# A spectral first stage: real bins folded into a product, projections turned by VectorE, weight conversion double-buffered

## The chip, the cores and the metric

The program runs on one core of one Trainium2 chip. The core has TensorE (PE in the profile; PEld is its weight load), VectorE (DVE), ScalarE (ACT), GpSimd (POOL), and SyncE (SP), whose queue issues most of the DMA transfers. Each engine works through its own instructions in the order in which the program gives them. The metric is the device time of one execution, in microseconds; lower is better.

## The reference

Three layers follow each other. The input x has 8 batches of 3072 positions with 256 channels.

```
X  = rfft(x, axis=1)                                   # 1537 complex bins
Yr = soft(Xr @ w_r - Xi @ w_i + b_r)                   # soft(v) = sign(v) * max(|v| - 0.01, 0)
Yi = soft(Xr @ w_i + Xi @ w_r + b_i)
x  = irfft(Yr + 1j * Yi, n=3072).reshape(24576, 256)

logits = x @ phi                                       # 32 slots, 8 experts of 4 slots
slots  = softmax(logits, axis=0).T @ x                 # each slot: a mean over all tokens
slots  = relu(slots @ w1[e]) @ w2[e]                   # its expert
x      = softmax(logits, axis=1) @ slots

h   = x @ w_in                                         # 256 -> 2048
out = (h * tanh(softplus(h))) @ w_out                  # 2048 -> 256
```

moe2_w_in and moe2_w_out arrive as 64-bit floats, and the kernel converts them to 32-bit floats itself.

## The kernel before

The program has two halves. The last one, `ffn`, computes the third layer over all 24576 tokens and depends on the slots of all batches. The first half, which the change touches, computes the spectra, the logits and the slots. `body` writes it as small functions; each call gets a position by `at(position, function, ...)`, and all calls are issued sorted by position. That list sets the order on every engine. The unit of position is one k: there are 32 of them, four to a batch (k = 4b + g), each one 16 of a batch's 64 frequency groups. PSUM tiles come from one ring of eight buffers.

For one k the steps are these. `stage2` (position k - 1.1, thus two units ahead of what else is issued there) makes 768 spectral columns in four calls: 16 TensorE products into PSUM; ScalarE writes the rounded upper part `xh` and the real part, VectorE the rest `xl` and the sum of real and imaginary parts `xsum`. When half the channels are there, ScalarE rounds `xsum` and VectorE takes the rest, waiting for it. `linear` (k + i/6, i = 0 to 5, for two halves `eh` of the outputs) is the complex product done with three real ones, each of six matmuls; product m = 0 takes the sums and is kept in `k1`, and m = 1, 2 go through VectorE (`p` L247, `cl` L249) and GpSimd (L250) into the thresholded spectrum `yt`. `special` (k + 1.02, once in a batch) does bin 0 and the middle bin, which have no imaginary part and share one column: four more products for each `eh` from a tile `xs` of two columns, then three small VectorE operations.

`project` (k + 1.18) multiplies `yt` by `phi`, eight small products of 32 output rows. `ptrans` (k + 1.38) turns the result, `inv1` (k + 1.58) multiplies it by the inverse transform's first factor, and `uturn` (k + 1.78) turns that and sends it to DRAM as `udr`. Each turn is `turn`: two TensorE transposes into PSUM and a ScalarE copy out; `project` and `inv1` are each followed by a ScalarE copy too. `c_load` (4b + 4.78) reads `udr` back for a batch's logits `lps` at 4b + 5.17, from which softmax and slots follow. `ytrans` (L310) turns the spectrum itself for the slots.

Between these steps `conv` converts the 64-bit weights in 32 pieces; step 0 is the DMA load of a piece into `cvs` (one buffer), step 1 begins with VectorE's `cva` (L490) and GpSimd's `cvc` (L489). `xsplit` (L170, L171) prepares the input for `stage1` (L187) of the next batch.

Of the kernel before, what the change touches and what calls it, by code (L numbers as in the profile page):

```python
# [20 lines left out]
NP = 32  # L21
NS = 32
# [44 lines left out]
def body(ctx, tc, x, w_r, w_i, b_r, b_i, phi, w1, w2, w_in, w_out, cbig, ct, out, dbg=None, stop=False):  # L67
    nc = tc.nc
# [51 lines left out]
    x_t, b_t, xh_t, xl_t, xs_t, yt_t, y_t, pt_t, k1_t = {}, {}, {}, {}, {}, {}, {}, {}, {}  # L120
# [81 lines left out]
    def stage2(k, h, p0):  # L202
        b, g = divmod(k, 4)
        if h == 0 and p0 == 0:
            xh_t[k] = bp.tile([128, 2, 8, 3, 48], F32R, tag="xh", name="xh")
            xl_t[k] = bp.tile([128, 2, 8, 3, 48], F32R, tag="xl", name="xl")
            if g == 0:
                xs_t[k] = sm.tile([128, 2, 2], F32, tag="xs", name="xs")
# [4 lines left out]
        xh = xh_t[k][:, h, p0:p0 + 4, 0:2]  # L213
        nc.scalar.activation(out=xh, in_=ps, func=AF.Copy)  # L214
        if p0 == 0:
            k1_t["s", h] = lp.tile([128, 8, 48], F32, tag="xsum", name="xsum")
        xs = k1_t["s", h]
        nc.scalar.activation(out=xs[:, p0:p0 + 4], in_=ps[:, :, 0], func=AF.Copy)  # L218
        nc.vector.tensor_sub(xl_t[k][:, h, p0:p0 + 4, 0:2], ps, xh.bitcast(F32))  # L219
        nc.vector.tensor_add(xs[:, p0:p0 + 4], ps[:, :, 1], xs[:, p0:p0 + 4])  # L220
        if g == 0 and p0 == 0:
            nc.vector.tensor_copy(xs_t[k][:, h, :], ps[:, 0, 0:2, 47])
        if p0 == 4:
            xh = xh_t[k][:, h, :, 2]
            nc.scalar.activation(out=xh, in_=xs, func=AF.Copy)  # L225
            nc.vector.tensor_sub(xl_t[k][:, h, :, 2], xs, xh.bitcast(F32))

    def linear(k, eh, m):
# [5 lines left out]
        ps = psum([128, 8, 48], "l")  # L234
        es = slice(eh * 128, eh * 128 + 128)
        n = 0
        for h in range(2):
            for w, xx in ((wh, xh), (wh, xl), (wl, xh)):
                nc.tensor.matmul(ps, lhsT=w[:, h, es], rhs=xx[:, h, :, src, :], start=n == 0, stop=n == 5)  # L239
                n += 1  # L240
        if m == 0:
            k1_t[eh] = lp.tile([128, 8, 48], F32, tag="k1", name="k1")
            nc.scalar.activation(out=k1_t[eh], in_=ps, func=AF.Copy)
# [8 lines left out]
    def special(k, eh):  # L252
        ps = psum([128, 2], "sp")
        for n, (h, w) in enumerate(((0, 0), (0, 1), (1, 0), (1, 1))):
            nc.tensor.matmul(ps, lhsT=wsp["a"][w].bitcast(F32)[:, h, eh * 128:eh * 128 + 128], rhs=xs_t[k][:, h, :],
                             start=n == 0, stop=n == 3)
        cl = sm.tile([128, 2], F32, tag="cs", name="cs")
        nc.vector.tensor_scalar(cl, ps, tlo[:, 0, eh:eh + 1], thi[:, 0, eh:eh + 1], op0=ALU.max, op1=ALU.min)
        nc.vector.tensor_sub(cl, ps, cl)
        nc.vector.tensor_scalar(yt_t[k][:, eh, 0, :, 47], cl, 0.5, None, op0=ALU.mult)  # L260

    def project(k):
        yt = yt_t[k]
        ps = psum([128, 2, 96], "pp")
        for eh in range(2):
            for j in range(4):
                nc.tensor.matmul(ps[32 * j:32 * j + 32], lhsT=ph[:, eh, :],
                                 rhs=yt[:, eh, 2 * j:2 * j + 2].rearrange("p q r f -> p q (r f)"),
                                 start=eh == 0, stop=eh == 1, tile_position=(0, 32 * j))
        pt = cp.tile([128, 2, 96], F32, tag="pt", bufs=2, name="pt")  # L270
        nc.scalar.activation(out=pt, in_=ps, func=AF.Copy)
        pt_t[k] = pt

    def turn(src, tag):
        ps = psum([96, 2, 128], "tn")
        for i in range(2):
            nc.tensor.transpose(ps[:, i], src[:, i], ident)  # L277
        t = cp.tile([96, 2, 128], F32, tag=tag, bufs=2, name=tag)
        nc.scalar.activation(out=t, in_=ps, func=AF.Copy)
        return t  # L280

    def ptrans(k):
        pt_t[k] = turn(pt_t[k], "phat")

    def inv1(k):
        g = k % 4
        ps = psum([128, 2, 96], "iu")
        for i in range(2):
            for j in range(4):
                nc.tensor.matmul(ps[32 * j:32 * j + 32, i], lhsT=pt_t[k][:, i, 32 * j:32 * j + 32],  # L290
                                 rhs=t_t[:, 8 * g + 2 * j + i, :], start=True, stop=True, tile_position=(0, 32 * j))
        ut = cp.tile([128, 2, 96], F32, tag="pt", bufs=2, name="ut")
        nc.scalar.activation(out=ut, in_=ps, func=AF.Copy)
        pt_t[k] = ut

    def uturn(k):
        b, g = divmod(k, 4)
        u = turn(pt_t.pop(k), "u")
        if g == 0:
            udr[b] = dram.tile([NP, 96, NS], F32, tag="udr", bufs=2, name="udr")  # L300
        dst = udr[b][8 * g:8 * g + 8].rearrange("(j i) p s -> i p j s", i=2)
        for i in range(2):
            nc.sync.dma_start(out=dst[i], in_=u[:, i].rearrange("p (j s) -> p j s", s=NS))
# [548 lines left out]
```

## Time and profile before

| | |
|---|---|
| time before, median of 3 runs | 2021.65 us (2021.46 to 2022.32) |
| time of the profiled execution | 2021.28 us |
| its span, first to last instruction | 2019.5 us |
| TensorE busy | 1939.8 us (96%) |
| VectorE busy | 1302.8 us (65%) |
| ScalarE busy | 872.1 us (43%) |
| GpSimd busy | 269.8 us (13%) |
| mean granted TensorE clock | 0.979 |

The profiled execution lies 0.37 us under the median, and 1.78 us of it are outside the span. A share of the whole span mixes the first half, up to about 700 us, and `ffn`, which begins with its first product at 749.5 us. A matmul's end is modelled, so consecutive matmuls overlap in the rows: what one costs is the distance from its start to the next start.

### The profile page before, as it was taken

The numbers are of one execution on the slowest core, as the hardware profiler recorded it, in microseconds if no ns is written. First come the engines' busy times: TensorE is split into PE (matmuls) and PEld (weight loads), VectorE is DVE, ScalarE is ACT, GpSimd is POOL, SyncE is SP. The second block draws the span as 40 slices with busy tenths as digits, with TensorE's granted clock in tenths as the row PEclk, the third lists the DMA queues.
The fourth block names the chain that finished last, engine by engine and source line by source line (L and its number), as shares of the span: only waits on it lengthen the run. The fifth ranks groups of instructions, "written<-read, shape, count | busy, mean of one in ns | idle before, by whom it ended". The sixth has DMA issues, their size and how long they took to land.

```text
span 2019.5 us, 31863 instructions
## 1 busy us (share of the span) xinstructions
PE 1939.8 (96%) x12670; PEld 1645.8 (81%) x12670; DVE 1302.8 (65%) x2020; ACT 872.1 (43%) x1569; POOL 269.8 (13%) x289
## 2 busy tenths in 40 slices
PE   5899999999999878999999999999999999999999
PEld 3787787888888647888888888888888888888887
DVE  3777767678777525666666666666666666666665
ACT  4566565565655422333333333333333333333332
POOL 1444343434434100000000000000000000000000
PEclk8999999899999899999999999999999999999999
DMA  8665465656664591002002001002001002000000
GB/s 250 177 181 159 147 179 153 176 158 177 194 185 118 192 326 42 22 22 53 22 22 53 22 21 42 22 22 53 21 22 53 22 22 53 21 22 22 22 22 21
DMA packets 147716, 177.16 MB, mean 88 GB/s; under 512 B 57504, under 2 KB 102688, under 8 KB 147120
## 3 DMA queue, kind: packets, MB, share of 16 engines
q1 hardware_dynamic: 145776, 170.38, 28.5%
q0 software_dynamic: 1792, 4.76, 0.7%
q8 instruction: 100, 1.64, 0.4%
q14 instruction: 48, 0.39, 0.1%
HBM read 103.79 MB, written 71.30 MB: 87 GB/s over the span
## 4 chain that ended last, share of the span: by engine, by line
PE 66%; DMA 3%; DVE 2%; issue 1%; ACT 1%; POOL 0%; SPq 0%; POOLq 0%; DVEq 0%; ACTq 0%
PE o L792 53%; PE h L762 9%; PE l L239 2%; DMA whl<-whl_d 1%; PE s L211 1%; DMA c_d<-chl 0%; DMA raw<-in_moe_w_dram 0%; PE tr L310 0%; POOL yt L250 0%; PE dt L436 0%; DVE rm L333 0%; PE tn L277 0%; PE dps L402 0%; DMA v<-udr 0%; PE sps L457 0%
## 5 line engine op out<-in xcount | busy, mean ns | idle before, releaser
L792 PE MATMUL o<-whl,gh 128*128 128x512 f32 x3072 | 1084.3, 395 | 8.5 <-DMA whl<-whl_d 8.5
L792 PE MATMUL o<-whl,gl 128*128 128x256 f32 x3072 | 828.4, 280 | 0.0
L768 ACT ACTIVATE g<-h 128x1024 f32<-128x1024 f32 x384 | 394.1, 1027 | 760.2 <-PE h L762 754.1
L792 PEld LDWEIGHTS o<-whl,gh 128*128 128x128 f32 x3072 | 567.2, 188 | 130.5 <-issue 8.9
L792 PEld LDWEIGHTS o<-whl,gl 128*128 128x128 f32 x3072 | 579.2, 189 | 31.5
L773 DVE CAST gh<-g 128x1024 fp32r<-128x1024 f32 x384 | 265.3, 691 | 366.9 <-ACT g L768 366.9
L777 DVE TENSOR_TENSOR gl<-g,gh 128x1024 fp32r<-128x1024 f32 x384 | 469.8, 1224 | 28.9 <-DVE gh L773 0.9
L762 PE MATMUL h<-ctt,mst 128*128 128x512 f32 x768 | 241.0, 395 | 2.1 <-ACT g L768 1.4
L250 POOL TENSOR_TENSOR yt<-p,cl 128x384 f32<-128x384 f32 x126 | 134.1, 1064 | 223.4 <-DVE cl L249 116.0
L762 PEld LDWEIGHTS h<-ctt,mst 128*128 128x128 f32 x768 | 121.0, 188 | 21.0 <-ACT g L768 2.3
L211 PEld LDWEIGHTS s<-tall,bt 96*128 96x128 f32 x1024 | 125.5, 201 | 6.3 <-DMA bt<-sdr 5.6
L211 PE MATMUL s<-tall,bt 96*128 96x96 f32 x1024 | 125.5, 283 | 4.5 <-DMA bt<-sdr 4.5
L187 PE MATMUL s<-xsp,f1s 128*128 128x512 f32 x288 | 100.8, 452 | 29.3 <-ACT xsp L170 13.4
L800 DVE TENSOR_TENSOR os<-o,os 128x256 f32<-128x256 f32 x192 | 76.2, 417 | 77.3 <-ACT os L799 77.3
L187 PEld LDWEIGHTS s<-xsp,f1s 128*128 128x128 f32 x288 | 53.2, 202 | 52.1 <-ACT xsp L170 19.3
L249 DVE TENSOR_SCALAR cl<-p,tlo,thi 128x384 f32<-128x384 f32 x128 | 75.6, 591 | 25.0 <-POOL yt L250 14.5
L799 ACT ACTIVATE os<-o 128x256 f32<-128x256 f32 x192 | 73.4, 383 | 41.0 <-PE o L792 38.0
L247 DVE TENSOR_TENSOR p<-l,k 128x384 f32<-128x384 f32 x128 | 70.4, 550 | 26.1 <-PE l L239 24.9
L219 DVE TENSOR_TENSOR xl<-s,xh 128x384 fp32r<-128x384 f32 x128 | 70.4, 550 | 18.4 <-ACT xsum L218 16.2
L214 ACT ACTIVATE xh<-s 128x384 fp32r<-128x384 f32 x128 | 62.3, 487 | 32.3 <-PE s L211 32.3
L225 ACT ACTIVATE xh<-xsum 128x384 fp32r<-128x384 f32 x64 | 33.5, 524 | 98.7 <-DVE xsum L220 98.7
L312 ACT ACTIVATE y<-tr 96x512 f32<-96x512 f32 x128 | 66.8, 599 | 17.7 <-PE tr L310 17.6
(189 smaller groups left out, 1919.0 us busy)
## 6 DMA issues: line engine op xcount, KB each, us to landing
xc<-in_x_dram SPq DMA_DIRECT2D x96, 256.0 KB, 3.1
sdr<-a SPq DMA_DIRECT2D x96, 256.0 KB, 3.4
bt<-sdr SPq DMA_DIRECT2D x32, 768.0 KB, 7.3
out_dram<-os SPq DMA_DIRECT2D x48, 512.0 KB, 2.6
ctt<-c_d SPq DMA_DIRECT2D x32, 384.0 KB, 7.8
c_d<-chl SPq DMA_DIRECT2D x16, 384.0 KB, 3.3
w1t<-in_moe_w_dram SPq DMA_DIRECT2D x6, 1024.0 KB, 6.9
w2t<-in_moe_w_dram SPq DMA_DIRECT2D x5, 1024.0 KB, 10.4
```

Of the source, the lines that this page charges most:

```text
L187: nc.tensor.matmul(ps, lhsT=f1s[w], rhs=xs[:, v], start=n == 0, stop=n == 2)
L211: nc.tensor.matmul(ps[:, i], lhsT=b_t[k][:, p0 + i, h * 128:(h + 1) * 128], rhs=t_m[:, 8 * g + p0 + i, :], start=True, stop=True)
L219: nc.vector.tensor_sub(xl_t[k][:, h, p0:p0 + 4, 0:2], ps, xh.bitcast(F32))
L249: nc.vector.tensor_scalar(cl, p, tlo[:, ri, eh:eh + 1], thi[:, ri, eh:eh + 1], op0=ALU.max, op1=ALU.min)
L250: (nc.vector if k == NK - 1 and m == 2 else nc.gpsimd).tensor_sub(yt[:, eh, :, ri, :], p, cl)
L762: nc.tensor.matmul(ps[:, i], lhsT=mst[:, f * 128:f * 128 + 128], rhs=ct_t[b][:, 4 * m:4 * m + 4].rearrange("p n t -> p (n t)"), start=True ...
L768: nc.scalar.activation(out=g, in_=h_t.pop(p), func=AF.Mish)
L773: nc.vector.tensor_copy(gh, g)
L777: nc.vector.tensor_sub(gl, g, gh.bitcast(F32))
L792: nc.tensor.matmul(o, lhsT=a[:, i, ts], rhs=w, start=f == 0 and n == 0, stop=f == 15 and n == 1)
L799: nc.scalar.activation(out=os[:, t], in_=ps[:, 1], func=AF.Copy)
L800: nc.vector.tensor_add(os[:, t], ps[:, 0], os[:, t])
```

## The change

Three edits, all in the first half.

1. The two real bins ride in the product of the sums. The tiles `xh`, `xl` are laid out by source (`NC` = 384 columns each of real, imaginary and sum), the sums have two more columns for the first unit of a batch, and `linear` with m = 0 multiplies 386 columns there. `special` reads the two columns from `k1`, without products of its own, and stands at k + 0.98 and 0.99.
2. `project` makes an output of 96 rows (three row blocks `a` of 32 frequencies) by 8 groups of 32 slots, with six products of 256 columns in place of eight of 192. One VectorE transpose of 32x32 blocks reads it from PSUM and writes `phat`; a second one does the same behind `inv1`. `turn`, `ptrans`, `uturn` and four ScalarE copies go. `inv1` stands at k + 1.48, and `udr` is written by four DMAs of 32 partitions, not two of 96.
3. `cvs` has two buffers, and step 0 of `conv` stands 0.45 of a piece ahead of step 1's piece (a piece is 0.953 units), where it stood 0.02 of a unit ahead. The tile `cvf` goes; `cva` takes its place.

```
     def linear(k, eh, m):
...
+        w = NC + 2 if m == 0 and k % 4 == 0 else NC
+        full = psum([128, NC + 2], "l")
+        ps = full[:, 0:w]
+        cs = slice(src * NC, src * NC + w)
...
-                nc.tensor.matmul(ps, lhsT=w[:, h, es], rhs=xx[:, h, :, src, :], start=n == 0, stop=n == 5)
+                nc.tensor.matmul(ps, lhsT=ww[:, h, es], rhs=xx[:, h, cs], start=n == 0, stop=n == 5)
...
     def special(k, eh):
-        ps = psum([128, 2], "sp")
-        for n, (h, w) in enumerate(((0, 0), (0, 1), (1, 0), (1, 1))):
-            nc.tensor.matmul(ps, lhsT=wsp["a"][w].bitcast(F32)[:, h, eh * 128:eh * 128 + 128], rhs=xs_t[k][:, h, :],
-                             start=n == 0, stop=n == 3)
+        v = k1_t[eh][:, NC:NC + 2]
...
     def project(k):
         yt = yt_t[k]
-        ps = psum([128, 2, 96], "pp")
+        ps = psum([96, 8, NS], "pp")
         for eh in range(2):
-            for j in range(4):
-                nc.tensor.matmul(ps[32 * j:32 * j + 32], lhsT=ph[:, eh, :],
-                                 rhs=yt[:, eh, 2 * j:2 * j + 2].rearrange("p q r f -> p q (r f)"),
-                                 start=eh == 0, stop=eh == 1, tile_position=(0, 32 * j))
-        pt = cp.tile([128, 2, 96], F32, tag="pt", bufs=2, name="pt")
-        nc.scalar.activation(out=pt, in_=ps, func=AF.Copy)
-        pt_t[k] = pt
...
+            v = yt[:, eh].rearrange("p q r f -> p q (r f)")
+            for a in range(3):
+                nc.tensor.matmul(ps[32 * a:32 * a + 32], lhsT=ph[:, eh, :], rhs=v[:, :, 32 * a:32 * a + 32],
+                                 start=eh == 0, stop=eh == 1, tile_position=(0, 32 * a))
+        pt_t[k] = cp.tile([96, 8, NS], F32, tag="phat", bufs=2, name="phat")
+        nc.vector.transpose(out=pt_t[k].rearrange("p q s -> p (q s)"), in_=ps.rearrange("p q s -> p (q s)"))
 
     def inv1(k):
...
-        ut = cp.tile([128, 2, 96], F32, tag="pt", bufs=2, name="ut")
-        nc.scalar.activation(out=ut, in_=ps, func=AF.Copy)
...
+        u = cp.tile([128, 2, 3, NS], F32, tag="u", bufs=2, name="u")
+        nc.vector.transpose(out=u.rearrange("p i a s -> p (i a s)"), in_=ps.rearrange("p i f -> p (i f)"))
...
-        for i in range(2):
-            nc.sync.dma_start(out=dst[i], in_=u[:, i].rearrange("p (j s) -> p j s", s=NS))
+        for j in range(4):
+            q = 8 * g + 2 * j
+            nc.sync.dma_start(out=udr[b][q:q + 2].rearrange("i (a n) s -> n i a s", n=32), in_=u[32 * j:32 * j + 32])
...
-            src = cvp.tile([128, n, 2], I32, tag="cs", name="cvs")
-            nc.sync.dma_start(out=src, in_=srcd[i])
-            cv.update(lo=src[:, :, 0].bitcast(U32), hi=src[:, :, 1])
+            cv["n"] = cvp.tile([128, n, 2], I32, tag="cs", bufs=2, name="cvs")
+            nc.sync.dma_start(out=cv["n"], in_=srcd[i])
...
-            at(k + 1.02, special, k, 0)
-            at(k + 1.03, special, k, 1)
+            at(k + 0.98, special, k, 0)
+            at(k + 0.99, special, k, 1)
         at(k + PA["pj"], project, k)
-        at(k + PA["pj"] + 0.2, ptrans, k)
-        at(k + PA["pj"] + 0.4, inv1, k)
-        at(k + PA["pj"] + 0.6, uturn, k)
+        at(k + PA["pj"] + 0.3, inv1, k)
...
-        at(sp * i - 0.02, conv, s_, d_, ii, 0)
+        at(sp * (i - 0.45), conv, s_, d_, ii, 0)
```

How this moves instructions is shown for unit k = 21, a second unit of a batch. On TensorE before, between `project` (`pp`) and the inverse product (`iu`) stood the transposes of the spectrum (`tr`), three groups of matmuls of `linear` (`l`), one of `stage1` (`s`), and the turn `tn`:

```order
L267 MATMUL pp<-yt,ph 32x192 x8
L310 MATMUL tr<-cb,yt 96x128 x16
...
L277 MATMUL tn<-cb,pt 96x128 x2
L187 MATMUL s_6341<-xsp,f1s_113 128x512
...
L436 MATMUL dt<-tall,dd 32x96 x8
L239 MATMUL l<-xh,ah 128x384
...
L436 MATMUL dt<-tall,dd 32x96 x8
L290 MATMUL iu<-tall,phat 32x96 x8
```

The same place of the changed kernel:

```order
L274 MATMUL pp<-yt,ph 32x256 x6
L300 MATMUL tr<-cb,yt 96x128 x16
L248 MATMUL l<-xh,ch 128x384
...
L248 MATMUL l<-xh,cl 128x384
L188 MATMUL s_6036<-xsp,f1s_113 128x512
...
L426 MATMUL dt<-tall,dd 32x96 x8
L285 MATMUL iu<-tall,phat 32x96 x8
L248 MATMUL l<-xh,ah 128x384
```

The turn is gone, and `iu` has moved ahead of the next six `l`; only one group of `l` and what stands with it now lies between `pp` and `iu`. On VectorE before, this unit's stretch ended the work of `stage2` (`xl`, `xsum`) and went on with two steps of `conv`, `p`, `cl` and more conversion:

```order
L226 TENSOR_TENSOR xl<-xsum,xh 128x8x48
L490 TENSOR_SCALAR cva<-cvs 128x256
L492 SCALAR_TENSOR_TENSOR cvb<-cvs,cva 128x256
L247 TENSOR_TENSOR p<-l,k_6245 128x384
L249 TENSOR_SCALAR cl<-p,tlo,thi 128x384
L494 SCALAR_TENSOR_TENSOR cvf<-cvc,cvb 128x256
```

The same place of the changed kernel:

```order
L232 TENSOR_TENSOR xl<-xsum,xh 128x384
L480 TENSOR_SCALAR cva<-cvs 128x256
L482 SCALAR_TENSOR_TENSOR cvb<-cvs,cva 128x256
L256 TENSOR_TENSOR p<-l,k_5946 128x384
L258 TENSOR_SCALAR cl<-p,tlo,thi 128x384
L277 STREAM_TRANSPOSE phat<-pp 96x256
L484 SCALAR_TENSOR_TENSOR cva<-cvc,cvb 128x256
L256 TENSOR_TENSOR p<-l,k_5946 128x384
L258 TENSOR_SCALAR cl<-p,tlo,thi 128x384
```

The transpose that `iu` needs stands behind `cl` of the next unit's first product, and so behind all of the work of `stage2` before it.

## Rows read from the trace of the kernel before

**Rows 1.** Stretch: length, busy PE, PEld, DVE, ACT, POOL, granted clock, DMA share, GB/s.

```profile
62.00:678.00 616.00, 588.28 (x5050) 503.59 (x5049) 464.79 (x964) 358.09 (x892) 262.07 (x277) 0.97 0.58 165
```

**Rows 2.** TensorE's waits, 62 to 678 us: total us, times, longest.

```profile
PE s L187 <- DVE xsp L171: 4.3, 3, 3.3
PE mt L340 <- DVE rm L335: 3.9, 4, 1.2
PE pp L267 <- DVE yt L260: 3.5, 2, 1.8
...
PE tn L277 <- ACT ut L293: 2.1, 1, 2.1
...
PE iu L290 <- ACT phat L279: 1.6, 1, 1.6
```

**Rows 3.** TensorE in order of time, the products of special (L255).

```profile
309.72 0.28 PE L255 MATMUL sp<-xs,ah 128*128 128x2 f32 x2
...
311.42 0.42 PE L239 MATMUL l<-xh,bh 128*128 128x384 f32 x1
```

**Rows 4.** TensorE in order of time around one turn (L277).

```profile
675.53 0.39 PE L277 MATMUL tn<-cb,ut 128*96 128x128 f32 x2
675.67 0.42 PE L239 MATMUL l<-xh,ch 128*128 128x384 f32 x1
675.93 0.34 PE L239 MATMUL l<-xl,ch 128*128 128x384 f32 x1
676.12 0.34 PE L239 MATMUL l<-xh,cl 128*128 128x384 f32 x1
```

**Rows 5.** TensorE in order of time, two kinds of products of 32 output rows.

```profile
335.45 0.86 PE L267 MATMUL pp<-yt,ph 128*32 128x192 f32 x16
...
683.37 3.66 PE L457 MATMUL sps<-y,dh 96*32 96x256 f32 x64
```

**Rows 6.** Groups of VectorE instructions by line: busy us, mean ns.

```profile
L220 DVE TENSOR_TENSOR xsum<-s,xsum 128x192 f32<-128x192 f32 x128 | 44.2, 345 | 0.0
...
L800 DVE TENSOR_TENSOR os<-o,os 128x256 f32<-128x256 f32 x192 | 76.2, 417 | 77.3 <-ACT os L799 77.3
...
L498 DVE SCALAR_TENSOR_TENSOR cvc<-cvs,cva 128x256 f32<-128x256 uint32 x32 | 19.7, 615 | 0.3
```

**Rows 7.** What VectorE waited for from 62 to 678 us.

```profile
DVE xl L226 <- ACT xh L225: 36.0, 61, 0.6
DVE cva L490 <- DMA cvs<-in_moe_w_in_dram: 25.4, 10, 3.9
...
DVE cva L490 <- DMA cvs<-in_moe_w_out_dram: 8.6, 6, 4.7
```

**Rows 8.** In order of time, TensorE's last `l`, `dt`, and VectorE's `cl`, in two units.

```profile
133.70 0.34 PE L239 MATMUL l<-xh,cl 128*128 128x384 f32 x1
...
133.73 0.48 DVE L249 TENSOR_SCALAR cl<-p,tlo,thi 128x384 f32<-128x384 f32 x1
...
656.78 0.34 PE L239 MATMUL l<-xh,cl 128*128 128x384 f32 x1
...
657.99 0.54 PE L436 MATMUL dt<-tall,dd 96*32 96x96 f32 x16
...
658.82 0.48 DVE L249 TENSOR_SCALAR cl<-p,tlo,thi 128x384 f32<-128x384 f32 x1
```

**Rows 9.** In order of time, one wait for a conversion load and the matmul behind it.

```profile
385.08 0.29 DVE L490 TENSOR_SCALAR cva<-cvs 128x256 int32<-128x256 int32 x1 [4.69 <-DMA cvs<-in_moe_w_out_dram]
...
388.22 0.80 PE L187 MATMUL s<-xsp,f1s 128*128 128x512 f32 x1 [3.29 <-DVE xsp L171]
```

**Rows 10.** Busy time by stretches, behind that wait; the columns of Rows 1.

```profile
387.00:407.30 20.30, 19.08 (x72) 17.84 (x72) 11.87 (x28) 5.55 (x14) 6.07 (x7) 0.50 0.50 134
```

**Rows 11.** The chain that ended last, behind the last unit's `project`.

```profile
679.22 0.57 PE pp L267 x8
...
683.05 0.33 SPq L303
```

More of the change, by code (lines that the diff above doesn't have):

```diff
@@ L21 @@
 NP = 32
+NC = 384
 NS = 32
@@ L212, in stage2, with part @@
                              start=True, stop=True)
-        xh = xh_t[k][:, h, p0:p0 + 4, 0:2]
+        def part(t):
+            v = t[:, h, 0:2 * NC].rearrange("p (r q f) -> p q r f", r=2, f=48)
+            return v[:, p0:p0 + 4]
+        xh = part(xh_t[k])
         nc.scalar.activation(out=xh, in_=ps, func=AF.Copy)
         if p0 == 0:
-            k1_t["s", h] = lp.tile([128, 8, 48], F32, tag="xsum", name="xsum")
+            k1_t["s", h] = lp.tile([128, NC + 2], F32, tag="xsum", name="xsum")
         xs = k1_t["s", h]
-        nc.scalar.activation(out=xs[:, p0:p0 + 4], in_=ps[:, :, 0], func=AF.Copy)
-        nc.vector.tensor_sub(xl_t[k][:, h, p0:p0 + 4, 0:2], ps, xh.bitcast(F32))
-        nc.vector.tensor_add(xs[:, p0:p0 + 4], ps[:, :, 1], xs[:, p0:p0 + 4])
+        xv = xs[:, 0:NC].rearrange("p (q f) -> p q f", f=48)[:, p0:p0 + 4]
+        nc.scalar.activation(out=xv, in_=ps[:, :, 0], func=AF.Copy)
+        nc.vector.tensor_sub(part(xl_t[k]), ps, xh.bitcast(F32))
+        nc.vector.tensor_add(xv, ps[:, :, 1], xv)
         if g == 0 and p0 == 0:
-            nc.vector.tensor_copy(xs_t[k][:, h, :], ps[:, 0, 0:2, 47])
+            nc.vector.tensor_copy(xs[:, NC:n], ps[:, 0, 0:2, 47])
         if p0 == 4:
-            xh = xh_t[k][:, h, :, 2]
-            nc.scalar.activation(out=xh, in_=xs, func=AF.Copy)
-            nc.vector.tensor_sub(xl_t[k][:, h, :, 2], xs, xh.bitcast(F32))
+            xh = xh_t[k][:, h, 2 * NC:2 * NC + n]
+            nc.scalar.activation(out=xh, in_=xs[:, 0:n], func=AF.Copy)
+            nc.vector.tensor_sub(xl_t[k][:, h, 2 * NC:2 * NC + n], xs[:, 0:n], xh.bitcast(F32))
     def linear(k, eh, m):
@@ L237, in linear @@
         for h in range(2):
[L238 to L239 removed]
+            for ww, xx in ((wh, xh), (wh, xl), (wl, xh)):
+                nc.tensor.matmul(ps, lhsT=ww[:, h, es], rhs=xx[:, h, cs], start=n == 0, stop=n == 5)
                 n += 1
         if m == 0:
[L242 to L243 removed]
+            k1_t[eh] = lp.tile([128, NC + 2], F32, tag="k1", name="k1")
+            nc.scalar.activation(out=k1_t[eh][:, 0:w], in_=ps, func=AF.Copy)
             return
```

48 lines of the change are left out of this document (17 added, 31 removed).

## The prediction

> **What bounds the kernel now.** I read the busy time by stretches first. From 62 to 678 us, the part of the first half in which units follow each other, TensorE is busy for 588.28 of 616.00 us, VectorE for 464.79 and ScalarE for 358.09 [rows 1]. So TensorE sets the end of this stretch, and of the stretch behind it too: `ffn` cannot begin before the last batch's slots. What TensorE's stream loses here, the end loses, one for one. The rest of TensorE's time, 27.7 us, is waiting, and the waits show for whom: mostly VectorE (`xsp`, `rm`, `yt`), some ScalarE in the two turns (`ut`, `phat`) [rows 2]. VectorE is nearer to its limit than its busy time tells: it also sits idle for 36.0 us inside `stage2`, where `xl` waits for ScalarE's rounding, and for 25.4 + 8.6 = 34.0 us at the head of conversion pieces, where `cva` waits for its load [rows 7]. Taken together it is occupied for 535 of 616 us, and it lags behind TensorE in bursts. A unit lasts 616.00 / 31 = 19.9 us, since 31 projections lie in this stretch.
>
> **What goes from TensorE.** Products of `special`: from their first row to the next `l` it is 311.42 - 309.72 = 1.70 us [rows 3], eight times: **-13.6 us**. In their place 12 matmuls in a batch have 386 columns in place of 384, some 0.01 us in all by the 0.19 us that one takes. Turns: the two transposes cost 675.67 - 675.53 = 0.14 us, and the matmul behind them 0.26 us to its successor in place of the 0.19 of the one after it [rows 4], thus 0.21 us for each of 64 turns: **-13.4 us**. The transposes' own busy time overlaps with their neighbours and is not what they cost.
>
> **What TensorE gets.** `project` goes from four rounds of four 192-column products (eight, in two passes each; 0.86 us with the tail) to four rounds of three 256-column ones. The nearest row with 256 columns is `sps`: 64 in 3.66 us, 0.229 us for a round of four [rows 5]. Lower bound 4 x 0.229 = 0.91 us, that is +0.05; upper bound the ratio of columns, 0.86 x 256 / 192 = 1.15, that is +0.29. I take the middle, +0.17 us, for 31: **+5.3 us** (bounds 1.6 and 9.0). The sum for TensorE's own work is -21.7 us.
>
> **What VectorE gets.** Two transposes for each unit, out of PSUM, of 256 and 192 columns. The trace has no VectorE transpose. By rows with as many columns and a PSUM operand they take 417 and 345 ns; the slowest row of 256 columns, 615 ns, bounds both from above, and below the 345 of the smaller one there is no reason to go [rows 6]. I take 0.76 us for a unit, 23.6 us in the stretch. ScalarE's four copies go; it was not the bound, and what their absence brings is the wait for ScalarE in the turns [rows 2]. For this transpose only the Trainium skill has a price: VectorE: DVE Perf Modes, section "The three transpose paths", gives 311 ns for 128x128 bf16, which by its 0.96 GHz clock and one column a cycle I estimate as 0.44 and 0.38 us here, 25.5 us in all; no run here shows it yet, and the sum would not change by it.
>
> VectorE gives back more than that: the load of `cvs` now leaves about 0.45 x 0.953 + 0.11 = 0.53 units (10.6 us) ahead of `cva`, where it left 0.13 units (2.5 us) ahead, and the second buffer lets it. The 34.0 us of waits [rows 7] should all but go. SP issues two DMAs more in a unit, by 0.33 us each [rows 11]; behind them in its queue are the loads `xc`, which are two steps of `stage1` ahead of their use and hide them. Without that cover it would be 0.7 us a unit.
>
> **The new wait.** `iu` needs `phat`, and `phat` now stands in VectorE's queue behind `xl`, `xsum` of `stage2` and `p`, `cl` of the next unit. On TensorE only `tr`, six `l` and in some units `s` and `dt` stand between `pp` and `iu`. Who waits behind it: all of TensorE. I compared in every unit when TensorE is through with these (what stands before `iu` now) and when VectorE is through with `cl`, plus 0.45 us for the transpose. In ten of the units between k = 3 and k = 29 VectorE is later. In k = 3 the last `l` starts at 133.70 and has its 0.19, and `cl` ends at 134.21: 0.8 us late. In k = 29 the last `l` starts at 656.78, `dt` then takes some 0.5, and `cl` ends at 659.30: 2.3 us [rows 8]. Over the ten it is 14.4 us. All are second and fourth units of a batch; in the first and third TensorE has softmax or slot products there as well. Two corrections about cancel: in three of the ten, 4.9 of the 14.4 us, a conversion wait stands shortly before, while TensorE comes earlier and VectorE has more to do in the second units, whose first unit holds the softmax reductions. So **+14.4 us**, bounds 0 and twice that. In the first units `mt` already waits for VectorE's `rm` [rows 2]; there TensorE arrives 1.7 us earlier for lack of `special`, and in half of the batches, where no conversion wait held VectorE up, that is lost again: **+5 us** with the edge of what `phat` adds.
>
> **Waits that go.** Behind conversion loads: the 3.3 of `xsp` and the 3.5 of `yt`; of the turns the 2.1 and 1.6 [rows 2]: **-10.5 us**. All waits together: +8.9 us.
>
> **The clock.** At 385.08 VectorE had waited 4.69 us for a load, and TensorE for that 3.29 us [rows 9]; behind it TensorE's granted clock is 0.50, thus 1.2 GHz, until 407.3 us, where 2.4 GHz is full speed [rows 10]. TensorE was busy for 19.08 us in these 20.30, so that full clock would have saved near half, 9.5 us. With the load early this cause goes, but a wait for `phat` may do the same elsewhere; I count half, **-5 us**.
>
> **Behind the last unit** the chain from `pp` to the `udr` transfer holds two turns and two copies: 683.05 - 679.22 = 3.8 us [rows 11], of which `iu` and `pp` are 1.2. Two transposes replace 2.6 us by 0.8, and two more DMA issues of 0.33 us come last: **-1 us**.
>
> **Sum.** -13.6 - 13.4 + 5.3 + 8.9 - 5 - 1 = -18.8 us on the profiled 2021.28 us; from the median, 0.37 higher, 2002.9 us. I predict **2003 us**. A change under 0.2% (4 us) is about what a measurement of this kernel cannot tell from none.
>
> **Rivals.**
>
> *The clock pays for the new wait.* A wait of 2 to 3 us in the second units is as long as the one that was followed by 20.30 us at 0.50 [rows 9, 10]. If two such stretches come and none goes, the clock costs +19 in place of -5: 2027 us; with one, 2013 to 2018 us. For it: the length. Against: the mean granted clock of the whole stretch is 0.97 [rows 1], so most waits were followed by no drop. The Trainium skill, TensorE: Matmul & The Clock Gate, section "HAM oscillation — how this bites in real kernels", says that idle gaps between bursts put the clock back to half; by that rule this rival gains, and the one stretch shown agrees.
>
> *VectorE's queue becomes the bound (slower).* If `iu` waits w us in every one of the 31 units, the sum without the clock is -21.7 - 1 - 10.5 + 31 w; it turns positive at w = 1.07 us. At 1.5 us it is +13.3: 2035 us. For it: VectorE's 535 us, less 34.0, plus 23.6, are 524 of the 594 us that TensorE would leave, and if a transpose took twice its price, 548. Against: my ten units are a third of all, a mean of 0.46 us, and each wait lets VectorE catch up.
>
> *The waits vanish (faster).* If the early loads leave VectorE no backlog at `stage2`, `iu` waits for nothing and the low stretch goes: -21.7 - 1 - 10.5 - 9.5 = -42.7: 1979 us. For it: 34.0 us of idle time given back against 23.6 of work. Against: ten lags remain of which only three have a load wait ahead.
>
> *The loads come no earlier* because SP reaches them late: waits stay, -21.7 - 1 + 14.4 + 5 - 3.7 (the turns' waits) = -7.0: 2015 us.
>
> **Chances.** The forecast, 1992 to 2010 us: 0.58. Waits vanish, below 1992: 0.20. Clock or loads, 2010 to 2017.6: 0.10. Between 2017.6 and 2025.7: 0.04. Slower by VectorE's queue or by two low stretches: 0.08. So faster 0.88, same 0.04, slower 0.08. The range takes three quarters of the case below and most of that above: 1982 to 2016 us; the forecast's own is 1992 to 2010.
>
> **What would show it.** In the trace after: no L255 products, no wait of `cva` for a load, VectorE's transposes at 0.35 to 0.62 us, `pp` rounds of 0.22 us and more, and under TensorE's waits a new line, `iu` for `phat`, of about 14 us in second and fourth units. The last projection should come some 18 us earlier. It is wrong if that line exceeds 35 us, if transposes take twice the price, or if the granted clock is low for much more than before.

## The result, and the profile after

The changed kernel is slower, not faster: a median of 2037.29 us in five runs (2035.45 to 2040.26), beside 2021.46 us for the kernel before (2013.80 to 2022.32). The ratio is 1.0084, 95% interval 1.0060 to 1.0109. The forecast was 2003 us, its range 1982 to 2016. The profiled execution took 2035.45 us.

The stretch from 62 to 678 us of the kernel after, by windows (columns as in [rows 1]):

```profile
62.00:678.00 616.00, 560.59 (x4530) 467.69 (x4529) 484.90 (x1009) 328.53 (x759) 256.46 (x271) 0.96 0.56 160
```

TensorE's busy time falls from 588.28 to 560.59 us, but fewer units fit into the stretch. The last `project` began at 678.67 us before:

```profile
678.67 1.08 PE L267 MATMUL pp<-yt,ph 128*32 128x192 f32 x16
```

and begins at 694.93 after:

```profile
694.93 1.31 PE L274 MATMUL pp<-yt,ph 128*32 128x256 f32 x12
```

So TensorE has less to do, and waits longer than it saved. The longest of its waits from 62 to 678 us, after (total us, times, longest):

```profile
PE iu L285 <- DVE phat L277: 18.2, 10, 4.3
PE pp L274 <- DVE yt L266: 15.3, 8, 3.1
PE tr L300 <- DVE xsum L226: 5.9, 8, 1.0
PE s L188 <- POOL xsp L172: 3.0, 7, 0.7
PE mt L330 <- DVE rm L325: 2.6, 2, 1.3
```

The first line is the wait that the prediction priced at 14.4 us. The second stood at 3.5 us [rows 2] and was to go; it is now there in every batch. TensorE's waits, 54.3 us in all, are mostly for VectorE. (`mt`, met below too, is the product that turns the softmax's maxima `rm`.) VectorE's own waits, after:

```profile
DVE xl L232 <- ACT xh L231: 36.6, 62, 0.6
DVE xl L225 <- ACT xsum L224: 36.1, 64, 0.9
DVE p L256 <- PE l L248: 18.3, 19, 2.8
```

The conversion loads have gone from the list, as forecast (34.0 us in [rows 7]). In their place, and just as long, stands a line that the prediction does not have: `xl` of `stage2`, the first kind (L225), 36.1 us in 64 waits. The same is seen on ScalarE:

```profile
ACT xh L219 <- DVE xl L225: 58.4, 53, 3.3
ACT xh L231 <- DVE xsum L226: 55.0, 62, 0.9
```

`xh` of the one half waits for `xl` of the other, although they write different columns of different tiles. In order of time, one `stage2` of the kernel after, first the products (TensorE) and ScalarE:

```profile
505.30 3.62 PE L211 MATMUL s<-tall,bt 96*128 96x96 f32 x31
...
510.37 0.49 ACT L219 ACTIVATE xh<-s 128x384 fp32r<-128x384 f32 x1 [1.88 <-DVE xl L225]
510.76 0.32 ACT L224 ACTIVATE xsum<-s 128x192 f32<-128x192 f32 x1
```

VectorE in the same `stage2`:

```profile
509.73 0.55 DVE L225 TENSOR_TENSOR xl<-s,xh 128x384 fp32r<-128x384 f32 x1
510.19 0.35 DVE L226 TENSOR_TENSOR xsum<-s,xsum 128x192 f32<-128x192 f32 x1
511.11 0.56 DVE L225 TENSOR_TENSOR xl<-s,xh 128x384 fp32r<-128x384 f32 x1 [0.57 <-ACT xsum L224]
511.59 0.34 DVE L226 TENSOR_TENSOR xsum<-s,xsum 128x192 f32<-128x192 f32 x1
512.52 0.56 DVE L232 TENSOR_TENSOR xl<-xsum,xh 128x384 fp32r<-128x384 f32 x1 [0.59 <-ACT xh L231]
```

Read it as a ladder: VectorE's first `xl` ends at 510.28; only then does ScalarE begin the second `xh`, after 1.88 us of idle time, though the products that it reads were through at 508.92 (505.30 + 3.62); and only behind that, at 511.11, can VectorE's second `xl` begin. VectorE loses 0.57 us here, twice in a unit, in the middle of its burst.

The instruction stream says why. ScalarE's rows there in the kernel after; in the brackets are the engines whose semaphores an instruction waits for:

```
400 L219 ACTIVATE xh<-s_4350 128x4x2x48 [waits DVE_49,PE_49]
403 L219 ACTIVATE xh<-s_4361 128x4x2x48 [waits PE_49]
405 L219 ACTIVATE xh<-s_4371 128x4x2x48 [waits DVE_49,PE_49]
```

Every second `xh` waits for a VectorE semaphore; in the kernel before all of them waited for PE_49 alone. With the columns of `xh` in the order source, block, frequency the two halves that `stage2` writes lie between each other (columns 0-191 and 384-575 against 192-383 and 576-767). They do not share a column, but the waits that the program was built with take them as overlapping: the second write of `xh` must wait for the reader of the first, which is VectorE's `xl`.

### The profile page after: what moved, and what is told of

The parts are those of the page before. It is cut to its first block, busy times and chain, and to the rows that moved or that the text cites. A ratio compares the mean times of both kernels' runs of the same rounds, so it can differ in the third digit from the quotient of the medians.

```text
span 2033.7 us, 31162 instructions
## 1 busy us (share of the span) xinstructions
PE 1927.2 (95%) x12286; PEld 1622.7 (80%) x12286; DVE 1333.6 (66%) x2084; ACT 845.4 (42%) x1441; POOL 270.3 (13%) x289
## 4 chain that ended last, share of the span: by engine, by line
PE 66%; DMA 3%; DVE 2%; ACT 1%; issue 1%; SPq 0%; POOL 0%; DVEq 0%; ACTq 0%; POOLq 0%
PE o L780 53%; PE h L750 9%; PE l L248 2%; DMA whl<-whl_d 1%; PE s L211 1%; DMA raw<-in_moe_w_dram 0%; DMA c_d<-chl 0%; PE tr L300 0%; DVE p L256 0%; DVE xl L225 0%; PE dt L426 0%; DVE rm L323 0%; PE pp L274 0%; PE iu L285 0%; ACT xh L219 0%
## 5 line engine op out<-in xcount | busy, mean ns | idle before, releaser
L225 DVE TENSOR_TENSOR xl<-s,xh 128x384 fp32r<-128x384 f32 x128 | 71.1, 555 | 52.1 <-ACT xsum L224 50.7
L300 PE MATMUL tr<-cb,yt 128*96 128x128 f32 x512 | 71.9, 293 | 6.3 <-DVE xsum L226 5.9
L300 PEld LDWEIGHTS tr<-cb,yt 128*96 128x96 f32 x512 | 59.6, 135 | 22.7 <-issue 9.3
```

The costliest lines, as they stand in the source:

```text
L300: nc.tensor.transpose(ps[:, i, eh], yt[:, eh, 2 * c + i].rearrange("p r f -> p (r f)"), ident)
```

## The experiments

Fifteen kernels, in four groups of three or four; each group ran on one chip together with the kernel before, whose medians there were 2022.87 (e1 to e4), 2023.15 (e5 to e8), 2019.46 (e9 to e12) and 2022.17 us (e13 to e15). The ratio is to the kernel before of the same group; differences in us are between medians. Where two kernels are of different groups, so of different chips, their ratios are the safer comparison, and a difference of a few us between them is not much above the noise.

| kernel | bins | turns | loads | median us | ratio to before, 95% interval |
|---|---|---|---|---|---|
| after | yes, with the wait | both | yes | 2037.29 | 1.0084 (1.0060 to 1.0109) |
| e1 | yes, no wait | both | yes | 1998.64 | 0.9885 (0.9858 to 0.9911) |
| e2 | layout with the wait | - | - | 2054.78 | 1.0155 (1.0129 to 1.0182) |
| e8 | layout without the wait | - | - | 2020.20 | 0.9986 (0.9967 to 1.0005) |
| e3 | - | both | - | 2041.51 | 1.0099 (1.0072 to 1.0125) |
| e4 | - | both | yes | 1999.32 | 0.9880 (0.9857 to 0.9904) |
| e5 | - | - | yes | 1992.77 | 0.9853 (0.9825 to 0.9881) |
| e7 | yes, no wait | - | - | 2022.50 | 1.0003 (0.9988 to 1.0018) |
| e9 | yes, no wait | - | yes | 1993.71 | 0.9865 (0.9836 to 0.9893) |
| e6 | e1, special earlier | both | yes | 2009.18 | 0.9939 (0.9914 to 0.9963) |
| e10 | - | u alone | yes | 1992.96 | 0.9860 (0.9833 to 0.9888) |
| e11 | e9, split on GpSimd | - | yes | 2004.81 | 0.9914 (0.9882 to 0.9945) |
| e12 | - | both, inv1 later | yes | 1999.30 | 0.9897 (0.9866 to 0.9927) |
| e13 | e9, special on GpSimd | - | yes | 1987.16 | 0.9834 (0.9814 to 0.9853) |
| e14 | e1, special on GpSimd | both | yes | 1985.97 | 0.9829 (0.9807 to 0.9850) |
| e15 | as e13 | u alone | yes | 1985.82 | 0.9815 (0.9792 to 0.9838) |

### The added wait: e1, e2, e8

Theory 1 is the wait between `xh` and `xl`. Its rivals are VectorE's queue with the transposes in it (theory 2), and the three-wide `project` with the clock (theory 3). e1 takes the cause of the wait away from the changed kernel: the columns are ordered so that each half is one run.

```diff
-            v = t[:, h, 0:2 * NC].rearrange("p (r q f) -> p q r f", r=2, f=48)
+            v = t[:, h, 0:2 * NC].rearrange("p (q r f) -> p q r f", r=2, f=48)
...
+        def cols(t, h):
+            if m == 0:
+                return t[:, h, 2 * NC:2 * NC + w]
+            return t[:, h, 0:2 * NC].rearrange("p (q r f) -> p q r f", r=2, f=48)[:, :, src]
```

> The changed kernel, with the columns of a row of xh and xl in the order frequency block, source, frequency in place of source, frequency block, frequency (the sums and the two extra columns stay at the end). The two halves that stage2 writes no longer lie between each other, and in the instruction stream ScalarE's second xh then no longer waits for VectorE's first xl. Theory 1 (this wait, which the trace after shows as 58.4 us of ScalarE's idle time in xh and 15.9 us in xl, is what the forecast missed): the time falls by 15 to 30 us from 2037, to 2007 to 2022 us, the wait of xh for xl is gone from the trace, and the last projection comes at least 12 us earlier. Theory 2 (VectorE's queue, with the transposes in it, is the bound): within 6 us of 2037. Theory 3 (the three-wide project costs 11 us in place of 5, the rest is the clock): within 6 us of 2037.

Measured: 1998.64 us, **38.7 us faster** than the changed kernel, beyond what theory 1 expected. The waits are gone; VectorE in one `stage2` of e1:

```profile
520.39 0.56 DVE L225 TENSOR_TENSOR xl<-s,xh 128x384 fp32r<-128x384 f32 x1
520.87 0.35 DVE L226 TENSOR_TENSOR xsum<-s,xsum 128x192 f32<-128x192 f32 x1
521.13 0.55 DVE L225 TENSOR_TENSOR xl<-s,xh 128x384 fp32r<-128x384 f32 x1
521.60 0.35 DVE L226 TENSOR_TENSOR xsum<-s,xsum 128x192 f32<-128x192 f32 x1
522.53 0.56 DVE L232 TENSOR_TENSOR xl<-xsum,xh 128x384 fp32r<-128x384 f32 x1 [0.59 <-ACT xh L231]
```

The instructions last as long as before; only the gap is gone. Up to the start of the last `project`, thus for the same work, the kernel after and then e1:

```profile
62.00:694.93 632.93, 577.52 (x4681) 481.39 (x4679) 495.55 (x1027) 333.81 (x772) 262.55 (x277) 0.96 0.56 160
```

```profile
62.00:656.12 594.12, 563.85 (x4689) 473.56 (x4688) 488.89 (x1025) 327.74 (x769) 261.92 (x276) 0.99 0.60 170
```

The stretch is 38.8 us shorter, as much as the whole kernel gained. TensorE is busy for 13.7 us less with the same products, at a granted clock of 0.99 in place of 0.96, and its waits fall from 54.3 to 29.5 us, by 24.8. So about a third of the price of the added wait came with the clock, which was lower in the kernel that waits more; e1 changes nothing but the columns.

e2 puts the wait, alone, into the kernel before: a flat row by source, with two columns that nobody uses.

```diff
-            xh_t[k] = bp.tile([128, 2, 8, 3, 48], F32R, tag="xh", name="xh")
-            xl_t[k] = bp.tile([128, 2, 8, 3, 48], F32R, tag="xl", name="xl")
+            xh_t[k] = bp.tile([128, 2, 1154], F32R, tag="xh", name="xh")
+            xl_t[k] = bp.tile([128, 2, 1154], F32R, tag="xl", name="xl")
...
+        def part(t):
+            v = t[:, h, 0:768].rearrange("p (r q f) -> p q r f", r=2, f=48)
+            return v[:, p0:p0 + 4]
```

> The kernel before, with nothing of the change but rows of xh and xl that are laid out by source in a flat row of 1154 columns (two of them unused); special, project, the turns and the loads are as before. ScalarE's second xh then waits for VectorE's first xl, as in the changed kernel. Theory 1: slower than before by 15 to 30 us, 2036 to 2051 us, with a wait of xh for xl of about 50 us on ScalarE. Theories 2 and 3: within 5 us of the kernel before, 2016 to 2026 us.

e8 is e2 with rows of 1152:

```diff
-            xh_t[k] = bp.tile([128, 2, 1154], F32R, tag="xh", name="xh")
-            xl_t[k] = bp.tile([128, 2, 1154], F32R, tag="xl", name="xl")
+            xh_t[k] = bp.tile([128, 2, 1152], F32R, tag="xh", name="xh")
+            xl_t[k] = bp.tile([128, 2, 1152], F32R, tag="xl", name="xl")
```

> The second experiment's kernel with rows of 1152 columns in place of 1154 (the two were unused): the same layout by source and the same instructions, but in the instruction stream ScalarE's second xh does not wait for VectorE's first xl. If the wait is the cause: within 5 us of the kernel before, 30 us faster than with 1154 columns. If the layout by source itself is slow (the products' operands, the writes in two runs of 192): within 8 us of 2054.8.

Measured: e2 2054.78 us, slower than theory 1 expected too, and e8 2020.20 us. **Two unused columns cost 34.6 us** (two groups; the ratios are 1.0155 and 0.9986, the intervals far apart). In the instruction stream, e2 has the wait in every second `xh` and e8 has it in none of these; the computing instructions are the same. In e2 the second `xl` also waits for a semaphore of VectorE itself; no run took that away alone. VectorE's waits in e2, and then in e8:

```profile
DVE xl L224 <- ACT xsum L223: 37.3, 64, 0.9
DVE xl L232 <- ACT xh L231: 35.4, 60, 0.6
```

```profile
DVE xl L232 <- ACT xh L231: 36.6, 62, 0.6
```

This settles theory 1, though the wait cost more than the 15 to 30 us that it was given, and tells the wait from the layout: by source, without the wait, the kernel is as fast as before. Nor is it the length of the rows, for e1 has rows of 1154 columns as well. Why interleaved writes count as overlapping in rows of 1154 columns and not in rows of 1152 no run here shows.

### Each edit alone: e3, e4, e5, e7

Their edits are pieces of the change's own diff. e3 has its second edit alone (`project`, `inv1` and the two transposes), e4 the second and third, e5 the third alone (`conv`), e7 the first alone, in e1's columns. e5 and the kernels on it have one buffer less for `u`, for room:

```diff
-        t = cp.tile([96, 2, 128], F32, tag=tag, bufs=2, name=tag)
+        t = cp.tile([96, 2, 128], F32, tag=tag, bufs=2 if tag == "phat" else 1, name=tag)
```

> The kernel before with the second edit alone: project in three-wide rounds and the two turns by VectorE; special, the rows of xh and xl and the conversion loads are as before. By the sum of the prediction: turns -13.4, project +5.3 (measured after: +11.5), waits for phat +14.4 to +18.8, waits of the turns -3.7, together 0 to +13: 2021 to 2035 us. Theory 1: in this range, the lower half if VectorE has slack. Theory 2: above 2032 us, since VectorE has the transposes and still the load waits. Theory 3: 2024 to 2030 us.

> The kernel before with the second and the third edit: VectorE's turns and the conversion loads into a second buffer; special and the rows of xh and xl are as before. By the prediction's sum the loads take the 34 us of VectorE's load waits away and with them about 7 us of TensorE's waits and a low-clock stretch: 5 to 15 us faster than the kernel with the turns alone. Theory 1: faster than the kernel before by 0 to 12 us, 2009 to 2021 us, since only special's products are still to be saved. Theory 2: slower than the kernel before, above 2026 us. Theory 3: 2015 to 2025 us.

> The kernel before with the third edit alone, the early conversion loads into a second buffer (for room, u has one buffer in place of two). The prediction's terms for it: -6.8 us of TensorE's waits and half of the low-clock stretch, -5: 2005 to 2016 us. If VectorE's backlog sets the pace in the second units, as the kernel with turns but without the loads (2041.5) against that with both (1999.3) suggests, more: 1998 to 2010 us. If the loads matter only where VectorE has the turns as well: within 5 us of the kernel before.

> The kernel before with the first edit alone, in the columns of the first experiment (no added wait): the real bins as two columns of the first product, special without products. The prediction's term: -13.6 us, 2005 to 2011 us. If TensorE's time is only turned into a wait for VectorE, which the comparison of the first and fourth experiments suggests (-0.7 us): within 5 us of the kernel before.

Measured against before: turns alone +18.6 us, loads alone **-30.4**, turns and loads -23.6, bins alone **-0.6**. From these, in sequence: loads -30.4, turns on top of them +6.5 (between two groups, and the intervals of the ratios overlap), bins on top of both (e1 against e4) -0.7, the wait +38.7. e4 and e5 came out below every range that was expected of them.

The loads are worth two and a half times their term. Up to the last `project`, the kernel before and then e5:

```profile
62.00:678.67 616.67, 588.95 (x5056) 504.08 (x5054) 465.43 (x965) 358.76 (x893) 262.07 (x277) 0.97 0.58 165
```

```profile
62.00:651.57 589.57, 577.24 (x5081) 498.91 (x5080) 467.69 (x968) 360.80 (x898) 260.91 (x277) 0.99 0.62 173
```

Of the 27.1 us that the stretch is shorter, TensorE's waits are 15.0 (from 27.0 to 12.0) and its busy time 11.7, with the granted clock at 0.99 in place of 0.97. VectorE's load waits were 34.0 us [rows 7]; that the total is so close to them is in part the clock.

Turns alone come out as the theory of VectorE's queue expected (above 2032) and above what the other two did; the same theory is wrong for e4 (above 2026, measured 1999.32). What differs between the two is the loads. VectorE's waits in e3, of which the profiled execution, 2052.24 us, was the slowest of six:

```profile
DVE cva L474 <- DMA cvs<-in_moe_w_in_dram: 36.2, 13, 5.5
...
DVE cva L474 <- DMA cvs<-in_moe_w_out_dram: 21.4, 9, 4.7
```

The waits for loads grow from 34.0 to 57.6 us, for the loads stand in SP's queue behind `u`'s DMAs, and these now wait for VectorE (SP in e3):

```profile
SPq L287 <- DVE u L282: 79.6, 17, 17.3
```

That this queue is what delayed the loads is read from the trace; no run moved it by itself. e4, in which the loads have room, is 42.2 us faster than e3.

### Where the saved products of the bins go: e9, e6, e11, e13, e14

TensorE's four products per `eh` are gone in e7, in e1 and, beside the loads alone, in e9, and in none of them does the time fall against the kernel that has all but this edit.

> The kernel before with the first and the third edit (real bins in the first product, in columns by frequency; early conversion loads), turns as before; u has one buffer. With the loads alone TensorE waited only 12 us between 62 and 640 us, so TensorE is then what sets the pace. If so, the products of special, 13.6 us, come back in full: 1977 to 1983 us. If VectorE sets the pace of the second units even so, as with the turns (0.7 us came back): 1988 to 1995 us. Between them: VectorE's queue takes a part.

e9: 1993.71 us against 1992.77 of the loads alone. Up to the last `project`:

```profile
62.00:650.90 588.90, 563.37 (x4932) 480.59 (x4930) 466.43 (x965) 358.78 (x893) 260.78 (x277) 0.99 0.62 172
```

TensorE's busy time is 13.9 us below that of e5, as the prediction had it, and its waits are 25.0 us in place of 12.0: the saved time has become waiting. VectorE, then TensorE, at the end of one first unit of e9:

```profile
300.59 0.56 DVE L232 TENSOR_TENSOR xl<-xsum,xh 128x384 fp32r<-128x384 f32 x1 [0.59 <-ACT xh L231]
301.06 0.42 DVE L509 SCALAR_TENSOR_TENSOR cvc<-cvs,cvb 128x256 f32<-128x256 uint32 x1
301.40 0.28 DVE L269 TENSOR_SCALAR cs<-k,tlo,thi 128x2 f32<-128x2 f32 x1
...
302.99 0.17 DVE L271 TENSOR_SCALAR yt<-cs 128x2 f32<-128x2 f32 x1
303.10 0.56 DVE L261 TENSOR_TENSOR p<-l,k 128x384 f32<-128x384 f32 x1
```

```profile
300.32 1.16 PE L188 MATMUL s<-xsp,f1s 128*128 128x512 f32 x3
302.65 1.10 PE L278 MATMUL pp<-yt,ph 128*32 128x192 f32 x16 [1.17 <-DVE yt L271]
```

`special`'s six small operations stand at the end of VectorE's burst. The products that were removed had run on TensorE while VectorE worked this burst off; without them TensorE reaches `project` earlier, by up to the 1.70 us of [rows 3], and waits there for 1.17. Waits of this kind (`pp` for `yt`) are 3.9 us of the 25.0, in four batches; the rest is spread over other waits. Two edits try to give the time back. e6 puts `special` earlier in e1; e11 relieves VectorE in e9 of `xsp`:

```diff
-            at(k + 0.98, special, k, 0)
-            at(k + 0.99, special, k, 1)
+            at(k + 0.35, special, k, 0)
+            at(k + 0.85, special, k, 1)
```

> The kernel of the first experiment (columns by frequency) with special for the first channel half at k + 0.35 and for the second at k + 0.85 in place of k + 0.98 and k + 0.99, so that VectorE does it ahead of the next stage2 and not behind it. In the first experiment the projection of every first unit waits some 0.5 to 1.9 us for the yt that special writes. If this wait is where the saved products of special went (the kernel without the first edit is as fast, 1999.3 against 1998.6), 6 to 14 us faster than the first experiment: 1985 to 1993 us. If VectorE's whole work sets the pace of the second units, which is the same in either order: within 4 us of 1998.6.

```diff
-        (nc.gpsimd if b and j % 2 else nc.vector).tensor_sub(xs[:, 1], t, xs[:, 0].bitcast(F32))
+        (nc.gpsimd if b else nc.vector).tensor_sub(xs[:, 1], t, xs[:, 0].bitcast(F32))
```

> The kernel with bins and loads, with all subtractions of xsp behind the first batch on GpSimd (in place of every second one), which takes some 0.69 us from VectorE for each of 42 and costs GpSimd 1.35. If VectorE's queue takes back the gain of the bins, this gives it back: faster than the kernel with bins and loads by 5 to 12 us. If TensorE sets the pace there: within 3 us of it, or slower where the products of stage1 wait for GpSimd.

Both miss. e6 is 10.5 us slower than e1: the waits for `yt` go, but TensorE then waits for other things, among them `lps` for the load of `v`, and `mt`. Two of the waits of e6:

```profile
PE lps L320 <- DMA v<-udr: 7.0, 4, 2.4
PE mt L335 <- DVE rm L330: 6.8, 3, 2.8
```

The longest of these, 2.79 us in front of `mt` at 234.51 us, is followed by a granted clock of 0.50, thus 1.2 GHz:

```profile
234.70:241.40 6.70, 6.70 (x34) 5.66 (x34) 5.51 (x14) 2.01 (x4) 1.46 (x2) 0.50 0.39 111
```

The Trainium skill, TensorE: Matmul & The Clock Gate, section "HAM oscillation — how this bites in real kernels", says that bursts with idle gaps between them put the clock back to half; the row agrees, with 0.50 behind a gap of 2.79 us.

Yet the clock is not what e6 lost. Up to the last `project`:

```profile
62.00:665.81 603.81, 564.63 (x4680) 474.88 (x4678) 499.43 (x1026) 327.56 (x768) 260.06 (x277) 0.98 0.59 168
```

Beside e1 the busy time is 0.8 us longer and the waits 9.1 us (38.6 in place of 29.5). Which of the displaced waits is the first cause no run shows.

e11 is 11.1 us slower than e9: TensorE's `s` now waits 9.0 us for GpSimd's `xsp`, and one `lps` 3.8 us. It tells nothing on VectorE, since GpSimd became late in its place.

e13 (on e9) and e14 (on e1) move the six small operations to GpSimd, at the same position:

```diff
-        nc.vector.tensor_scalar(cl, v, tlo[:, 0, eh:eh + 1], thi[:, 0, eh:eh + 1], op0=ALU.max, op1=ALU.min)
-        nc.vector.tensor_sub(cl, v, cl)
-        nc.vector.tensor_scalar(yt_t[k][:, eh, 0, :, 47], cl, 0.5, None, op0=ALU.mult)
+        nc.gpsimd.tensor_scalar(cl, v, tlo[:, 0, eh:eh + 1], thi[:, 0, eh:eh + 1], op0=ALU.max, op1=ALU.min)
+        nc.gpsimd.tensor_sub(cl, v, cl)
+        nc.gpsimd.tensor_scalar(yt_t[k][:, eh, 0, :, 47], cl, 0.5, None, op0=ALU.mult)
```

> The kernel with bins and loads, with the three small operations of special for each channel half on GpSimd in place of VectorE, at the same place. There the projection of a first unit waited some 1.2 us for the yt that special writes at the end of VectorE's burst (2.60 to 3.16 us behind the rest of stage2), and VectorE's p came later by as much. If VectorE's backlog is where the saved products went, the waits of pp for yt go and 6 to 13 us come back: 1981 to 1988 us. If GpSimd is as late, or the next wait (lps for v, mt for rm) takes it: within 3 us of 1993.7.

> The kernel of the first experiment (all three edits, columns by frequency), special on GpSimd as in the run beside it. By the same argument, VectorE's backlog being larger with the transposes: 6 to 12 us faster than 1998.6, 1987 to 1993 us. If the next wait takes it, as it did when special was only put earlier (2009.2, with lps waiting for v and half-clock stretches behind): 1997 to 2010 us.

Measured: e13 1987.16 us, 6.5 under e9; e14 **1985.97 us, 12.7 under e1**. Both pairs are of two groups each: the ratios differ by 0.0031, with intervals that overlap, and by 0.0056, with intervals that do not. In e13 the same `project`, of k = 12, follows the products ahead of it with no wait:

```profile
298.89 1.16 PE L188 MATMUL s<-xsp,f1s 128*128 128x512 f32 x3
299.98 0.86 PE L278 MATMUL pp<-yt,ph 128*32 128x192 f32 x16
```

Up to the last `project` of e13:

```profile
62.00:644.42 582.42, 566.95 (x4949) 485.99 (x4949) 458.77 (x920) 359.26 (x896) 276.52 (x324) 0.99 0.62 175
```

TensorE's waits are 15.2 us, 9.8 under those of e9, and its busy time is 3.6 us above. So a time of the size of about half (e13) to most (e14) of the 13.6 us comes back when VectorE's queue is shorter at this place. That it is the bins' own saving is argued and not shown: no run relieves VectorE of `special` while its products stay on TensorE, and that might have given as much.

### The wait for phat, and what the turns are worth: e12, e10, e15

e12 puts `inv1` of e4 further behind `project`; e10 keeps the first turn as before and gives only the second to VectorE; e15 joins e13 with that.

```diff
-        at(k + PA["pj"] + 0.3, inv1, k)
+        at(k + PA["pj"] + 0.45, inv1, k)
```

> The kernel with turns and loads, with inv1 at 0.45 behind project in place of 0.3. The wait of iu for phat, 8.7 us there, should shrink below 4 us, since more of TensorE's work stands between. If that wait is what takes the turns' gain: 4 to 8 us faster than 1999.3, 1991 to 1995 us. If VectorE's work sets the pace, the wait shows up elsewhere (pp or mt for VectorE, lps for the load of v): within 3 us of 1999.3.

```diff
-        ut = cp.tile([128, 2, 96], F32, tag="pt", bufs=2, name="ut")
-        nc.scalar.activation(out=ut, in_=ps, func=AF.Copy)
...
+        u = cp.tile([128, 2, 3, NS], F32, tag="u", bufs=2, name="u")
+        nc.vector.transpose(out=u.rearrange("p i a s -> p (i a s)"), in_=ps.rearrange("p i f -> p (i f)"))
...
-        at(k + PA["pj"] + 0.6, uturn, k)
```

> The kernel before with the loads and half of the second edit: only the second turn, u, goes to VectorE, behind iu; project keeps its four-wide rounds and phat is turned by TensorE and ScalarE as before. In the kernel with both turns and the loads TensorE's own work fell by 9.9 us against the loads alone and its idle time rose by 9.8, of which 8.7 is the wait of iu for phat. If that wait is what takes the gain, this kernel, in which nobody on TensorE waits for the transpose, is faster than the loads alone by 3 to 8 us: 1985 to 1990 us. If VectorE's additional work is what costs, wherever it stands: 1991 to 1997 us.

> Bins, loads, special on GpSimd, and the second turn alone (u) by VectorE. The fastest parts together: if they add, 1980 to 1987 us; if something else holds all of them near 1993, as loads alone, bins and loads, and loads and u were all within 1 us of each other: 1990 to 1996 us.

Measured: 1999.30, 1992.96 and 1985.82 us. In e12 the wait of `iu` for `phat` falls from 8.7 us in e4 to 0.5, and the time does not move: the waits stand elsewhere, 27.2 us in all from 62 to 678 us in both. The longest of e12:

```profile
PE mt L324 <- DVE rm L319: 5.1, 4, 2.4
PE lps L309 <- DMA v<-udr: 4.9, 3, 2.7
PE s L187 <- DVE xsp L171: 3.6, 5, 1.3
```

Half the turns (e10) change nothing either, and in e15 nothing that its interval can tell from e13. With `special` on GpSimd the three kernels without turns, with `u` alone and with both lie within 1.4 us. The turns by VectorE are worth nothing that these runs can tell, in either direction, once VectorE is relieved. **e14 and e15 beat both kernels**, by some 36 us the kernel before and 51 the changed one.

## Why the prediction was wrong, point by point

**The step that failed: the change of layout was priced at nothing, without being priced.** "What VectorE gets" counts the transposes and the load waits, and the rivals count VectorE's time as 535 less 34.0 plus 23.6; no term stands for the new layout of `xh` and `xl` in `stage2`. There VectorE got a wait of 36.1 us. With it TensorE waited 24.8 us more and was busy 13.7 us longer, at a lower clock, than in e1; that the wait is the cause is shown by e1 (-38.7) and e2 against e8 (+34.6). The rival "VectorE's queue becomes the bound" names the right engine and, by luck, nearly the right time (2035 us at 1.5 us of wait in a unit), but its mechanism, `iu` waiting for `phat` in every unit, is not what happened: there were ten such waits, as forecast, of 18.2 us in all.

**The bound was wrong as a rule.** "What TensorE's stream loses here, the end loses, one for one" does not hold for work that TensorE gives up (13.6 us of products: -0.6), and not for one wait taken by itself (e12 beside e4, of two groups: 8.2 us of waits for `phat` gone, the time unchanged within the noise). Where VectorE lags in bursts, taking the lag away did move the end: 34.0 us of load waits, -30.4, and 36.1 us of added waits, 38.7. That both come out near one for one is no rule, for in each some 12 to 14 us came with the clock.

**Bins, -13.6.** TensorE's work fell; the end did not: -0.6, +0.9 and -0.7 us in three companies. In e9 the 13.9 us that went from TensorE's work came back as 13.0 us of waits: the products had run in a time in which TensorE would else have waited, in the unit shown for VectorE's burst. The prediction saw this only for half of the batches (+5 us).

**Turns, -13.4 + 5.3 + 14.4 - 3.7 = +2.6.** Measured +18.6 without the loads and +6.5 with them. `project` was priced well: a bounded middle of +0.17 us a unit, measured from 0.86 us [rows 5] to 1.06 us, at full clock, in the kernel after:

```profile
344.18 1.06 PE L274 MATMUL pp<-yt,ph 128*32 128x256 f32 x12
```

The transposes were priced at 0.76 us a unit and take 0.81; the groups after:

```profile
L277 DVE STREAM_TRANSPOSE phat<-pp 96x256 f32<-96x256 f32 x30 | 13.1, 437 | 0.0
...
L288 DVE STREAM_TRANSPOSE u<-iu 128x192 f32<-128x192 f32 x30 | 11.2, 374 | 0.2
```

The Trainium skill, VectorE: DVE Perf Modes, section "The three transpose paths", led to estimates of 0.44 and 0.38 us; the trace agrees, with 0.437 and 0.374.

**Loads, -6.8 and -5 of clock.** Measured -30.4: both terms were about half of what came, 15.0 us of waits and 11.7 us of busy time with the clock. The sum took only what TensorE was seen to wait for right behind loads, and one low stretch, and not what VectorE's lag cost elsewhere.

**Clock, -5.** The low stretch of [rows 10] did go (1.00 from 387.0 to 407.3 us after), but the mean fell from 0.97 to 0.96; in e1, without the added wait, it is 0.99 up to the last `project`. Of the rival that the clock pays for the new waits this much is right.

**Behind the last unit, -1.** From the start of the last `project` to the first product of `ffn` it was 749.5 - 678.67 = 70.8 us; after, `ffn` begins at 763.3: 68.4, thus -2.4.

The forecast's total is close to what the change does without its added wait (2003 against 1998.6), but that is luck, mainly two errors against each other: the loads' gain was put 18.6 us too low, that of the bins 13 us too high.

## What to carry to other kernels

A change of a tile's layout is a change of its waits: where two instructions write parts of one tile that lie between each other, read in the instruction stream which semaphores they and their readers now wait for, also on lines whose computation is the same. Two columns more in a row cost 34.6 us here, though `xh` and `xl` themselves took as long. And before a saving is counted on the busiest engine, look at what the other engine works off in that time: here, work that ran in the shadow of another engine's burst was free, and its removal became waits at later meeting points.

## What was unexpected in the hardware

Operations on two columns are not free. The six of `special` on VectorE took 1.76 us in a row in e9 (301.40 to 303.16), 0.16 to 0.58 each. GpSimd took 0.439 us for the first of the three in e13, on average over 16, and nobody waited for it:

```profile
L269 POOL TENSOR_SCALAR cs<-k,tlo,thi 128x2 f32<-128x2 f32 x16 | 7.0, 439 | 0.0
```

The two transposes differ by 63 ns for 64 columns, so I estimate some 1 ns a column; the two also differ in partitions (96 and 128), which no run separates.
